# Top-32 attention followed by a mixture of experts on one core: VectorE's steps of a tile ordered by a list scheduler, and the mask added on GpSimd in every third tile

## The chip, the core and the metric

The kernel runs on one core of a Trainium2 chip. The metric is device microseconds (us) of one execution; the runs before the change lie between 1251.29 and 1252.31 us. The engines are called as in the profile: PE (TensorE matmul, with PEld for its weight loads), DVE (VectorE), ACT (ScalarE), POOL (GpSimd) and SP (the engine that issues most DMAs).

## What is computed

For 8 batches of 8 heads, 576 x 576 attention scores are formed; in each row only the 32 largest count, the rest are masked before the softmax. The result, 4608 rows of 512, goes through a mixture of 8 experts of which each row takes one.

```python
scores = scale * np.matmul(q, k.transpose(0, 1, 3, 2))      # per head, 576 x 576
kth = np.partition(scores, -top_k, axis=-1)[..., -top_k:-top_k + 1]
scores = np.where(scores >= kth, scores, -1000000000.0)
attn = np.exp(scores - np.max(scores, axis=-1, keepdims=True))
attn = attn / (np.sum(attn, axis=-1, keepdims=True) + 1e-09)
x = attn @ v                                                # 4608 rows of 512 in all
...
e_idx = np.argmax(x @ w_gate + modality_bias[modality_id], axis=1)
for e in range(E):
    h = np.maximum(x[mask] @ w1[e], 0.0)
    out[mask] = gate_w[mask, None] * (h @ w2[e])
```

## The kernel before

The scores are cut into 288 tiles of 128 rows by 576 columns, nine for each pair of heads, 36 for each batch. One pass of the main loop, an iteration `i`, works on several tiles at different stages, and the order in which the code emits instructions is the order in which each engine executes them. In iteration `i`:

- PE forms the scores of tile `i+2` in PSUM (`qk`, L368) and transposes the probabilities of tile `i-9` (`trans`, L476); between these it multiplies by `v` (L504) and takes matmuls of the expert layer (L775, L787) from a queue. How many it takes is set by a credit, `spare_pe`, that grows by `STEP` in every iteration.
- ACT copies the scores to SBUF as `Ssb` (`sevac`, L373; there are ten such buffers, so tile `i+2` needs the buffer of tile `i-8`), computes a sign map `K` (`sign`, L412), exponentials (L436) and the evacuation of the transposes (L484).
- POOL multiplies scores by the sign map, `y` (`pool_y`, L418, tile `i-4`), and prepares small values (`n` L405, `sm` L399).
- DVE finds the threshold. For tile `i`, six MAX8 over 96 columns each give 48 candidates (`subs`, L380). For tile `i-1` a chain of five dependent steps takes the 24 largest of the candidates: MAX, MATCH_REPLACE, MAX, MATCH_REPLACE, MAX (`chain`, L391 to L393). For tile `i-5` one MAX8 over `y` gives the next 8 (`find`, L422). In every third iteration three small dependent steps, `eq`, `jk` and `kth`, select the threshold of three tiles (`pick`, L429 to L431). Steps of routing and of the experts' schedule (`small_`) and multiplications that read PSUM (`lo`) come in between. Last in the iteration, the mask is applied to tile `i-7`.

The mask has two forms. In the usual one ACT computes `ex` = exp of all scores (`expo`) and DVE keeps those at or over the threshold in one instruction with two SBUF tensors as inputs, which also sums them (`keep`, L442). A one-element POOL instruction that reads its result (`gate`, L465) stands ahead of POOL's `y`, so that `y` starts when `keep` has ended. In the other form, chosen by `early`, DVE writes a large negative number where the score is under the threshold (`hide`, L449, one tensor input), POOL adds it to the scores (`hidden`, L455, at the top of the next iteration), and ACT takes the exponential of that and sums (`masked`, L461). That form has no gate. Before, `early` holds for two of three of the first 48 tiles, 32 tiles in all; the map lies in `hT`, a buffer that the experts need later.

DVE's order in an iteration is made by hand: `weave` spreads the steps of `b_` (candidates, `find`, `lo`) evenly behind those of the chain, up to four steps of `b_` are held back (`HOLD`) to stand between the small and pick steps of `c_`, and the mask comes last.

After tile 287 the experts' last seven slots run alone, in a split form with three matmuls for each product.

Of the kernel before, what the change touches and what calls it, by code (L numbers as in the profile page):

```python
# [11 lines left out]
BF = mybir.dt.bfloat16  # L12
# [11 lines left out]
NB = 4  # L24
LX = 13
SN = 4
KB = 2
LOP = (2, 5, 8, 10, 12)
NW = 3
STEP = 3.25  # L30
STEPS = {"small": 0.1, "late": 0.5, "more": 0.15}
LJ = (5, 6)
PJ = (0, 1, 3)
VJ = 7
QL = 2
HOLD = 4
KW = 8
FILL = 6
KL = 2
# [1 line left out]
LT = LY + 1  # L41
# [20 lines left out]
END = (-3, 1.0)  # L62
SP_ = (0, 0, 0, 0, 0)
HUGE = float(2.0 ** 100)
EARLY = 48
EPS = 1e-9
KTH_MIN, KTH_MAX = 1e-18, float(2.0 ** 26)
XW = 516
# [4 lines left out]
def kernel(  # L73
# [14 lines left out]
    B, H, S, D = q.shape  # L88
# [20 lines left out]
    wk = att.enter_context(tc.tile_pool(name="wk", bufs=3))  # L109
# [83 lines left out]
    hT = const.tile([128, FC, SLOT], FT, name="hT")  # L193
# [76 lines left out]
    late, late_pe = [], []  # L270
# [106 lines left out]
    def subs(i):  # L377
        c = wk.tile([128, NSUB * 8], FT, name="cand", bufs=2)
        T[i]["c"] = c
        return [lambda s=s: V.max(c[:, s * 8:s * 8 + 8], T[i]["S"][:, bnd[s]:bnd[s + 1]]) for s in range(NSUB)]  # L380

    def chain(i):
        if i % 3 == 0:
            T[i]["mg"] = wk.tile([128, 3, 32], FT, name="mg", bufs=5)
        else:
            T[i]["mg"] = T[i - 1]["mg"]
        m = T[i]["mg"][:, i % 3]
        c = T[i]["c"]
# [31 lines left out]
    def find(i):  # L420
        t = T[i]
        V.max(t["mg"][:, i % 3, 24:32], t["y"])  # L422

    def pick(i):

        t = T[i]
        eq, v = (wk.tile([128, 3, 9], FT, name=nm, bufs=1) for nm in ("eq", "jk"))
        n = t["n"][:, 0, :]
        return [lambda: V.tensor_tensor(eq, i9s, n[:, :, None].to_broadcast([128, 3, 9]), op=OP.is_equal),  # L429
                lambda: V.tensor_tensor(v, eq, t["mg"][:, :, 23:32], op=OP.mult),  # L430
                lambda: V.tensor_reduce(kth[:, i - 2:i + 1], v, axis=AX.X, op=OP.add)]  # L431
# [6 lines left out]
    def keep(i, dn):  # L438

        t = T[i]  # L440
        probs(i)
        V.scalar_tensor_tensor(t["P"], t["S"], kth[:, i:i + 1], t["ex"], op0=OP.is_ge, op1=OP.mult, accum_out=dn)  # L442

    def hide(i):

        t = T[i]
        x = 2 * (i % 2)
        t["hb"] = hT[:, x:x + 2, :].rearrange("p f t -> p (f t)").bitcast(BF)[:, :S]
        V.tensor_scalar(t["hb"], t["S"], kth[:, i:i + 1], -HUGE, op0=OP.is_lt, op1=OP.mult)  # L449

    def hidden(i):
# [15 lines left out]
    def probs(i):  # L467

        c, h = divmod(role(i), 2)
        T[i]["P"] = Pm[:, :S] if c == 4 else Pb[c % 2][:, h * S:h * S + S]  # L470
# [15 lines left out]
    def av(p, j, x):  # L486

        vm, vt = LD[p]["v"]
        w = 256 if j < 8 else 64
        st = {}  # L490

        def part(c0, c1):
            if c0 == 0:
                st["po"] = psX.tile([128, 256], FT, name="X")
            po = st["po"]
            for c in range(c0, c1):
                for h in range(2):
                    l = vm[:, h, c, :] if c < 4 else vt[:, h if j < 8 else 2 * h, :]
                    if j < 8:
                        r = PT[:, j // 2 - 1:j // 2 + 1, c + 5 * h if c < 4 else 4, :]  # L500
                    else:
                        r = PT[:, 1, 4 + c, h * 64:h * 64 + 64]
                    o = po[h * 64:h * 64 + 64, :w]
                    PE.matmul(o.rearrange("p (a b) -> p a b", a=2) if j < 8 else o, l, r, start=(c == 0), stop=(c == 4))  # L504
            if c1 == 5:
                o = (j // 4) * 256
                xev.append(lambda: A.activation(x[:, o:o + w], po[:, :w], AF.Copy))
        cut = {3: AV3, 7: AV7, 8: (0, 5)}[j]
        return [((b - a) * COST["av" if j < 8 else "av8"], lambda a=a, b=b: part(a, b)) for a, b in zip(cut, cut[1:])]
# [118 lines left out]
    after = deque()  # L628
# [265 lines left out]
                rush.extend(pick + [begin] + rows + l1[:1] + done + [PAUSE, l1[1], PAUSE, l1[2], l1[3], PAUSE] + tok + go)  # L894
            side.extend(l2)

    def weave(a, b):

        nb, na, kb = len(b), len(a), 0
        for x in range(na):  # L900
            a[x]()
            e = (x + 1) * nb // na
            while kb < e:
                b[kb]()
                kb += 1
        while kb < nb:
            b[kb]()
            kb += 1

    def keep_warm(n):  # L910

# [8 lines left out]
    def bounds():  # L920

        bt = wk.tile([128, S], BF, name="K", bufs=KB).bitcast(FT)[:, :NT]
        V.tensor_scalar(bt, kth, KTH_MIN, 0.0, op0=OP.is_le, op1=OP.add, accum_out=bd_[:, 0:1])
        V.tensor_scalar(bt, kth, KTH_MAX, 0.0, op0=OP.is_ge, op1=OP.add, accum_out=bd_[:, 1:2])

    def beyond():

        bb = bd_.bitcast(BF)[:, 4:6]
        V.tensor_scalar(bb, bd_[:, 0:2], 0.0, None, op0=OP.is_gt)
        pbad = psX.tile([128, 2], FT, name="X")  # L930
        PE.matmul(pbad, onesb, bb, start=True, stop=True)
        V.tensor_reduce(bd_[:, 3:4], pbad, axis=AX.X, op=OP.add)
        V.tensor_copy(badi, bd_[0:1, 3:4])
# [14 lines left out]
            qk(0, 0, qbd[0])  # L948
        sevac(x)
    ok = lambda x: 0 <= x < NT  # L950
    early = lambda u: u < EARLY and u % 3 != 2
    dn_of = lambda u: den[(u // 36) % 2][:, (u // 9) % HP, role(u):role(u) + 1]
    PREP, PREP0 = dict(zip(PJ, "tkq")), dict(zip(PJ0, "tkq"))
    two = lambda nm, shape: [wk.tile(shape, FR, name=nm + x) for x in "hl"]
# [105 lines left out]
    for i in range(LAST):  # L1060
# [8 lines left out]
        p, j = divmod(i, 9)  # L1069
        u = i - TL  # L1070
# [14 lines left out]
        u = i - (KL + 1)  # L1085
# [6 lines left out]
        u = i - LE  # L1092
# [6 lines left out]
        u = i - TL  # L1099
        if ok(u):  # L1100
            evac(u)
        u = i - LR - 1
        if ok(u) and early(u):
            masked(u, dn_of(u))
        lo, lp = list(late), list(late_pe)
# [7 lines left out]
        part = (PREP if p else PREP0).get(j)  # L1113
# [54 lines left out]
        if i == NT + LR + 4:  # L1168
            beyond()
        spare_pe = min(spare_pe + (STEP if i < NT + TL + END[0] else END[1]) - cost, CAP)  # L1170
        while seen[0] and spare_pe > 0:
# [4 lines left out]
            c, f, new = moe[0]  # L1176
# [10 lines left out]
                nxt.append(lambda u=i + QL: sevac(u))  # L1187


        a_, b_, c_ = [], [], []  # L1190
        if ok(i):
            b_ += subs(i)
        if ok(i - 1):
            a_ += chain(i - 1)
        if ok(i - LT):
            b_.insert(2, lambda: find(i - LT))
            if (i - LT) % 3 == 2:
                c_ += pick(i - LT)
        for x, f in enumerate(lo):
            b_.insert(LOP[x] if x < len(LOP) else len(b_), f)  # L1200
        small_ = []
        for x in range(RN if rush else 0):
            f = rush.popleft() if rush else PAUSE
# [3 lines left out]
        if not small_:  # L1207
            while chore:
                small_.append(chore.popleft())
        for x in range(SN - len(small_)):  # L1210
            f = side.popleft() if side and not rush else PAUSE
# [1 line left out]
                break  # L1213
            small_.append(f)
        spare_pe += STEPS["small"] * len(small_) + (STEPS["late"] + STEPS["more"] * (len(lo) - 1) if lo else 0.0)
        for x, f in enumerate(small_):
            c_.insert(2 * x, f)
        if ok(i - LR):
            u = i - LR
            c_.append(lambda u=u: hide(u) if early(u) else keep(u, dn_of(u)))  # L1220

        if ok(i) and len(c_) > 1:
            n = min(len(c_) - 1, HOLD)
            held, b_ = b_[len(b_) - n:], b_[:len(b_) - n]
            m = len(c_) - n
            c_ = c_[:m] + [f for pair in zip(held, c_[m:]) for f in pair]
        weave(a_, b_)
        for f in c_:
            f()

        for f in moves:
            f()
# [19 lines left out]
        if i == CLOSE:  # L1252
# [5 lines left out]
            wk = att.enter_context(tc.tile_pool(name="tl", bufs=1))  # L1258
# [53 lines left out]
    wk = att.enter_context(tc.tile_pool(name="wkb", bufs=3))  # L1312
# [101 lines left out]
```

## Time and profile before

| | |
|---|---|
| median of 3 runs | 1251.63 us (1251.29 to 1252.31) |
| profiled execution, its own time | 1250.95 us |
| its span, first to last instruction | 1249.3 us |
| busy share of the span | PE 93%, DVE 90%, ACT 80%, POOL 53% |

A row of the profile's groups gives line, engine, operation, output<-input, count, then busy microseconds and mean nanoseconds of one. A row of the timeline gives start and duration in microseconds. An instruction's duration there includes the end of its pipeline, so that the next one can start before the duration is over: what an instruction costs its engine is the distance from its start to the next start.

### The profile page before, as it was taken

The page shows a single profiled execution, that of the slowest core. Times are in us where ns is not written, and L with a number is a line of the kernel's source. Part 1 is how long each engine was busy: PE and PEld are TensorE (multiplying, and loading weights), DVE is VectorE, ACT ScalarE, POOL GpSimd, SP SyncE. Part 2 cuts the span into 40 slices and gives each one's busy share as a digit, 9 for nine tenths or more (in the row PEclk, how much of TensorE's full clock was granted, in tenths as well). Part 3 has the DMA queues.
Part 4 walks back from the last instruction along what each step waited for, and adds up shares of the span by engine and source line. Part 5 has one row for each costly group of instructions (what it writes and reads, how often), then busy time and mean ns, then how long its engine had stood idle before and what let it go on. Part 6 is the DMA issues. An engine that isn't in the chain of part 4 may idle for free.

```text
span 1249.3 us, 28363 instructions
## 1 busy us (share of the span) xinstructions
PE 1167.8 (93%) x7998; PEld 918.1 (73%) x7998; DVE 1129.0 (90%) x5596; ACT 995.1 (80%) x2026; POOL 661.0 (53%) x1256
## 2 busy tenths in 40 slices
PE   8888887999998998999999999999999999999995
PEld 6666666777866877677776868777786866799895
DVE  6999999999999999999999999999999993667761
ACT  4999987889898988988899889978998873545542
POOL 4888866455474557554755566546655561110110
PEclk6999999999999999999999999999999999999998
DMA  4664337655347655665656567556663543757650
GB/s 96 152 182 101 85 85 206 167 158 167 85 135 210 195 148 145 172 175 146 185 151 180 135 172 192 149 145 177 190 169 101 158 142 116 268 199 257 220 180 15
DMA packets 204325, 197.12 MB, mean 158 GB/s; under 512 B 104413, under 2 KB 151533, under 8 KB 204160
## 3 DMA queue, kind: packets, MB, share of 16 engines
q1 hardware_dynamic: 196880, 175.92, 51.3%
q0 software_dynamic: 6080, 19.00, 4.2%
q8 instruction: 67, 1.10, 0.4%
q14 instruction: 98, 0.80, 0.2%
q10 hardware_dynamic: 1200, 0.30, 0.1%
HBM read 118.63 MB, written 24.23 MB: 114 GB/s over the span
## 4 chain that ended last, share of the span: by engine, by line
DVE 47%; PE 39%; ACT 4%; issue 3%; DMA 3%; POOL 2%; SPq 0%; POOLq 0%; ACTq 0%
DVE cand L380 12%; DVE mg L422 9%; DVE P L442 8%; PE E L787 7%; PE X L1024 5%; PE E L775 5%; PE X L1008 4%; PE X L504 4%; PE S L368 4%; PE T L476 3%; DVE cand L391 3%; DVE cand L392 3%; DVE mg L393 2%; DVE mg L391 2%; DVE mg L392 1%
## 5 line engine op out<-in xcount | busy, mean ns | idle before, releaser
L380 DVE MAX8 cand<-Ssb 128x8 f32<-128x96 f32 x1728 | 402.0, 247 | 6.8 <-ACT Ssb L373 6.8
L418 POOL TENSOR_TENSOR y<-Ssb,K 128x576 f32<-128x576 f32 x288 | 367.5, 1276 | 6.2 <-ACT K L412 6.0
L412 ACT ACTIVATE K<-Ssb,n 128x576 bf16<-128x576 f32 x288 | 229.1, 796 | 18.9 <-POOL y L418 17.6
L373 ACT ACTIVATE Ssb<-S 128x576 f32<-128x576 f32 x284 | 187.1, 659 | 68.7 <-PE S L368 28.3
L368 PE MATMUL S<-ks,qs 128*128 128x288 f32 x992 | 219.4, 343 | 22.5 <-ACT Ssb L373 20.1
L422 DVE MAX8 mg<-y 128x8 f32<-128x576 f32 x288 | 214.3, 744 | 1.3 <-POOL y L418 1.2
L368 PEld LDWEIGHTS S<-ks,qs 128*128 128x128 f32 x992 | 151.0, 190 | 73.7 <-ACT Ssb L373 39.2
L436 ACT ACTIVATE ex<-Ssb,sm 128x576 f32<-128x576 f32 x256 | 201.6, 788 | 0.0
L484 ACT ACTIVATE PT<-T 128x640 f32<-128x640 f32 (+1 forms) x288 | 192.5, 668 | 6.4 <-PE T L476 6.4
L775 PE MATMUL E<-xgT,w1b 128*128 128x256 f32 x768 | 187.4, 386 | 6.4 <-ACT hT L779 5.0
L442 DVE SCALAR_TENSOR_TENSOR P<-Ssb,kth,ex 128x576 f32<-128x576 f32 x230 | 190.9, 830 | 1.0 <-ACT ex L436 0.8
L476 PE MATMUL T<-idf,P 128*128 128x128 f32 x1152 | 169.8, 274 | 7.4 <-ACT P L461 6.7
L787 PE MATMUL E<-w2b,hT 128*128 128x512 f32 x368 | 173.6, 601 | 1.8 <-ACT hT L779 1.6
L775 PEld LDWEIGHTS E<-xgT,w1b 128*128 128x128 f32 x768 | 140.4, 191 | 29.4 <-ACT hT L779 9.1
L465 POOL TENSOR_SCALAR spare<-P 1x1 f32<-1x1 f32 x230 | 42.0, 182 | 223.7 <-DVE mg L391 184.7
L504 PE MATMUL X<-PT,vm 128*64 128x256 f32 (+1 forms) x1536 | 145.3, 331 | 4.0 <-ACT st L282 2.8
L476 PEld LDWEIGHTS T<-idf,P 128*128 128x128 f32 x1152 | 137.0, 140 | 15.1 <-ACT P L461 11.0
L504 PEld LDWEIGHTS X<-PT,vm 128*64 128x64 f32 x1536 | 87.5, 137 | 49.1 <-issue 9.2
L405 POOL TENSOR_SCALAR n<-mg 128x1 f32<-128x1 f32 x288 | 71.1, 247 | 73.6 <-DVE mg L393 60.0
L787 PEld LDWEIGHTS E<-w2b,hT 128*128 128x128 f32 x368 | 65.8, 192 | 57.8 <-issue 52.4
L1030 POOL DMA_INDIRECT out_dram<-ot,tk x14 | 14.0, 998 | 116.2 <-ACT ot L1029 116.2
L412 ACT ACTIVATION_READ_ACCUMULATOR K<-Ssb,n 128x1 f32 x288 | 62.7, 218 | 0.0
(235 smaller groups left out, 2285.5 us busy)
## 6 DMA issues: line engine op xcount, KB each, us to landing
w1b<-in_moe_w_dram SPq DMA_DIRECT2D x76, 512.0 KB
w2b<-in_moe_w_dram SPq DMA_DIRECT2D x76, 512.0 KB
ks<-st SPq DMA_DIRECT2D x62, 288.0 KB
ks<-st SPq DMA_DIRECT2D x62, 256.0 KB
qs<-st SPq DMA_DIRECT2D x124, 128.0 KB
xg<-xs SPq DMA_DIRECT2D x19, 516.0 KB
km<-in_k_dram SPq DMA_DIRECT2D x64, 128.0 KB
vm<-in_v_dram SPq DMA_DIRECT2D x32, 256.0 KB
```

The costliest lines, as they stand in the source:

```text
L368: PE.matmul(ps[:, hf, :288], l, m, start=(n == 0), stop=(n == len(terms) - 1))
L380: return [lambda s=s: V.max(c[:, s * 8:s * 8 + 8], T[i]["S"][:, bnd[s]:bnd[s + 1]]) for s in range(NSUB)]
L412: A.activation(t["K"], t["S"], AF.Sign, scale=2.0 ** -24 - 1.0, bias=t["n"][:, 1, i % 3:i % 3 + 1], accum_out=t["n"][:, 0, i % 3:i % 3 + 1])
L418: G.tensor_tensor(t["y"], t["S"], t["K"], op=OP.mult)
L422: V.max(t["mg"][:, i % 3, 24:32], t["y"])
L436: A.activation(t["ex"], t["S"], AF.Exp, bias=t["s"][:, i % 3:i % 3 + 1])
L442: V.scalar_tensor_tensor(t["P"], t["S"], kth[:, i:i + 1], t["ex"], op0=OP.is_ge, op1=OP.mult, accum_out=dn)
L476: PE.transpose(T[i]["pt"][:, x, :], (Pm if c == 4 else Pb[c % 2])[:, h * 512 + x * 128:h * 512 + x * 128 + 128], idf)
L484: A.activation(o, T[i]["pt"][:, :n], AF.Copy)
L504: PE.matmul(o.rearrange("p (a b) -> p a b", a=2) if j < 8 else o, l, r, start=(c == 0), stop=(c == 4))
L775: PE.matmul(ps[:, f % 2], w1b[:, c, f * 128:(f + 1) * 128], xgT[:, c, :], start=(c == 0), stop=(c == KC - 1))
L787: PE.matmul(o["py"], hT[:, f, t * 128:(t + 1) * 128], w2b[:, f, :], start=(f == 0), stop=(f == FC - 1))
```

## The change

A table `USE` gives for each kind of DVE step two numbers, the time that it holds the engine and the time until its result may be used; `FROM` gives a kind the earliest place in the iteration. `arrange` then picks, step by step, among the steps whose inputs are ready the one with the longest path behind it. The mask (`end`) stays last, and behind the pick and the chain's last step. `early` now holds for every third tile of all 288, 96 in all; the map has a buffer of its own, `hb`. `STEP` goes from 3.25 to 3.2.

```diff
+USE = {"part": (0.165, 0.25), "max": (0.11, 0.235), "drop": (0.19, 0.3), "find": (0.667, 0.8), "pick": (0.086, 0.21), "late": (0.6, 0.75), "small": (0.09, 0.24), "keep": (0.726, 0.85)}
+FROM = {"late": 0.7, "pick": 1.5}
...
-STEP = 3.25
+STEP = 3.2
...
-        x = 2 * (i % 2)
-        t["hb"] = hT[:, x:x + 2, :].rearrange("p f t -> p (f t)").bitcast(BF)[:, :S]
+        t["hb"] = wk.tile([128, S], BF, name="hb", bufs=1)
         V.tensor_scalar(t["hb"], t["S"], kth[:, i:i + 1], -HUGE, op0=OP.is_lt, op1=OP.mult)
...
+    def arrange(ops, *last):
+
+        left, t, path = list(ops), 0.0, {}
+        ops = ops + list(last)
+        for o in reversed(ops):
+            path[o] = o.delay + max([path[x] for x in ops if o in x.after], default=0.0)
+        while left or last:
+            if not left:
+                left, last = list(last), ()
+            free = [o for o in left if not any(x in left for x in o.after)]
+            now = [o for o in free if o.start <= t + EPS]
+            o = max(now, key=lambda o: path[o]) if now else min(free, key=lambda o: o.start)
+            left.remove(o)
+            t = max(t, o.start)
+            for x in left:
+                if o in x.after:
+                    x.start = max(x.start, t + o.delay)
+            t += o.use
+            o.f()
...
-    early = lambda u: u < EARLY and u % 3 != 2
+    early = lambda u: u % 3 == 0
...
+            ops += run(("max", "drop", "max", "drop", "max"), chain(i - 1))
+        cut_ = ops[-1:]
...
+            ops += [Op("part", f) for f in subs(i)]
...
+            found = Op("find", lambda: find(i - LT))
...
-        weave(a_, b_)
-        for f in c_:
-            f()
+            end.append(Op("keep", lambda: hide(u) if early(u) else keep(u, dn_of(u)), got, *cut_))
+        arrange(ops, *end)
```

The first place is DVE in the iteration that masks tile 174, in the experts' part of the loop; `mg` holds the values found, `cand` with a number the candidates with the larger ones replaced. Before:

```order
L391 MAX mg<-cand 128x8
L391 MATCH_REPLACE cand_10999<-mg,cand 128x48
L380 MAX cand<-Ssb 128x8
L392 MAX mg<-cand_10999 128x8
L392 MATCH_REPLACE cand_11000<-mg,cand_10999 128x48
L380 MAX cand<-Ssb 128x8
L393 MAX mg<-cand_11000 128x8
L422 MAX mg<-y 128x8
L429 TENSOR_TENSOR eq<-i9s,n 128x27
```

The same start of that iteration after the change (line numbers are one lower there):

```order
L390 MAX mg<-cand 128x8
L421 MAX mg<-y 128x8
L390 MATCH_REPLACE cand_11036<-mg,cand 128x48
L379 MAX cand<-Ssb 128x8
L391 MAX mg<-cand_11036 128x8
L379 MAX cand<-Ssb 128x8
L391 MATCH_REPLACE cand_11037<-mg,cand_11036 128x48
L428 TENSOR_TENSOR eq<-i9s,n 128x27
L379 MAX cand<-Ssb 128x8
L429 TENSOR_TENSOR jk<-eq,mg 128x27
L392 MAX mg<-cand_11037 128x8
```

Between each MAX and the MATCH_REPLACE that needs its result now stands a step that needs neither; the MAX over `y` has moved up to second place. Counted over the main loop, the first MATCH_REPLACE stood right behind its MAX in 146 of 288 iterations and the second one in 73; now that is so in 0 and 1. Pairs of dependent small steps with nothing between them go from 57 to 9.

The second place is POOL, four iterations at the same part of the program. Before:

```order
L405 TENSOR_SCALAR n<-mg 128x1
L399 TENSOR_SCALAR sm<-mg 128x3
L465 TENSOR_SCALAR spare<-P_119 1x1
L418 TENSOR_TENSOR y<-Ssb,K 128x576
L405 TENSOR_SCALAR n<-mg 128x1
L465 TENSOR_SCALAR spare<-P_120 1x1
L418 TENSOR_TENSOR y<-Ssb,K 128x576
```

And after the change:

```order
L404 TENSOR_SCALAR n<-mg 128x1
L398 TENSOR_SCALAR sm<-mg 128x3
L453 TENSOR_TENSOR ex<-Ssb,hb 128x576
L417 TENSOR_TENSOR y<-Ssb,K 128x576
L404 TENSOR_SCALAR n<-mg 128x1
L463 TENSOR_SCALAR spare<-P_120 1x1
L417 TENSOR_TENSOR y<-Ssb,K 128x576
```

In one iteration of three the gate is replaced by a whole 128x576 addition, and `y` stands behind that. On PE, ACT and SP the kinds and counts stay, but for the exponentials that change form with the mask and six of PE's filler matmuls. The expert matmuls that PE has been given by tile 280 number 688 before and 684 after, counting a 512-wide one twice.

## Rows read from the trace of the kernel before

**Rows 1.** The page, parts 1 and 4: busy time, and the chain that ended last.

```profile
PE 1167.8 (93%) x7998; PEld 918.1 (73%) x7998; DVE 1129.0 (90%) x5596; ACT 995.1 (80%) x2026; POOL 661.0 (53%) x1256
...
DVE 47%; PE 39%; ACT 4%; issue 3%; DMA 3%; POOL 2%; SPq 0%; POOLq 0%; ACTq 0%
```

**Rows 2.** Busy time of each engine in stretches of the span, instructions in brackets.

```profile
39.00:151.00 112.00, 99.11 (x807) 77.70 (x805) 111.59 (x589) 105.58 (x239) 94.81 (x128) 0.99 0.51 133
...
221.00:1017.00 796.00, 764.12 (x5197) 587.63 (x5193) 783.09 (x4144) 699.73 (x1444) 463.34 (x918) 1.00 0.59 160
1017.00:1249.00 232.00, 216.88 (x1353) 183.30 (x1353) 138.46 (x357) 111.09 (x178) 35.88 (x80) 0.98 0.52 177
```

**Rows 3.** Waits of DVE: total us, times, longest us.

```profile
DVE cand L380 <- ACT Ssb L373: 6.8, 6, 2.2
...
DVE mg L422 <- POOL y L418: 1.2, 3, 0.6
```

**Rows 4.** Timeline of DVE, two iterations side by side, from 229 us.

```profile
229.41 0.19 DVE L391 MAX8 mg<-cand 128x8 f32<-128x48 f32 x1
229.54 0.23 DVE L380 MAX8 cand<-Ssb 128x8 f32<-128x96 f32 x1
...
230.03 0.18 DVE L392 MAX8 mg<-cand 128x8 f32<-128x48 f32 x1
230.14 0.73 DVE L422 MAX8 mg<-y 128x8 f32<-128x576 f32 x1
...
231.73 0.79 DVE L442 SCALAR_TENSOR_TENSOR P<-Ssb,kth,ex 128x576 f32<-128x576 f32 x1
...
232.45 0.20 DVE L391 MAX8 mg<-cand 128x8 f32<-128x48 f32 x1
232.68 0.09 DVE L391 MATCH_VALUE_LOAD cand<-mg,cand 128x8 f32 x1
```

**Rows 5.** Timeline of DVE, the experts' small steps, without and with a step between.

```profile
538.05 0.17 DVE L659 MAX8 s_m<-s_key 128x8 f32<-128x8 f32 x1
538.25 0.23 DVE L670 TENSOR_SCALAR s_oh<-s_key,s_m 128x8 f32<-128x8 f32 x1
...
495.85 0.17 DVE L659 MAX8 s_m<-s_key 128x8 f32<-128x8 f32 x1
495.93 0.24 DVE L380 MAX8 cand<-Ssb 128x8 f32<-128x96 f32 x1
```

**Rows 6.** Timeline of all engines from 100 us: both forms of the mask, and POOL.

```profile
100.94 0.70 DVE L449 TENSOR_SCALAR hT<-Ssb,kth 128x576 bf16<-128x576 f32 x1
...
103.03 1.29 POOL L418 TENSOR_TENSOR y<-Ssb,K 128x576 f32<-128x576 f32 x1
...
103.87 1.06 DVE L442 SCALAR_TENSOR_TENSOR P<-Ssb,kth,ex 128x576 f32<-128x576 f32 x1
...
107.59 0.50 DVE L449 TENSOR_SCALAR hT<-Ssb,kth 128x576 bf16<-128x576 f32 x1
...
108.01 0.20 DVE L391 MAX8 mg<-cand 128x8 f32<-128x48 f32 x1
...
108.18 1.29 POOL L455 TENSOR_TENSOR ex<-Ssb,hT 128x576 f32<-128x576 f32 x1 [0.47 <-DVE hT L449]
...
109.43 1.29 POOL L418 TENSOR_TENSOR y<-Ssb,K 128x576 f32<-128x576 f32 x1
```

**Rows 7.** Timeline of POOL and of DVE at 878 us.

```profile
878.63 1.27 POOL L418 TENSOR_TENSOR y<-Ssb,K 128x576 f32<-128x576 f32 x1
...
878.77 1.74 DVE L442 SCALAR_TENSOR_TENSOR P<-Ssb,kth,ex 128x576 f32<-128x576 f32 x1
```

**Rows 8.** Groups by line on ACT: the sum that the other mask form reads out.

```profile
L461 ACT ACTIVATION_READ_ACCUMULATOR P<-ex,sm 128x1 f32 x26 | 5.9, 226 | 0.0
```

**Rows 9.** Timeline of PE: transposes, and the group that starts behind them.

```profile
617.19 0.71 PE L476 MATMUL T<-idf,P 128*128 128x128 f32 x5
617.65 0.48 PE L281 MATMUL X<-st,nid 128*128 128x512 f32 x1
```

More of the change, by code (lines that the diff above doesn't have):

```diff
@@ L26 @@
 SN = 4
+USE = {"part": (0.165, 0.25), "max": (0.11, 0.235), "drop": (0.19, 0.3), "find": (0.667, 0.8), "pick": (0.086, 0.21), "late": (0.6, 0.75), "small": (0.09, 0.24), "keep": (0.726, 0.85)}
+FROM = {"late": 0.7, "pick": 1.5}
 KB = 2
-LOP = (2, 5, 8, 10, 12)
 NW = 3
-STEP = 3.25
+STEP = 3.2
 STEPS = {"small": 0.1, "late": 0.5, "more": 0.15}
@@ L35 @@
 QL = 2
-HOLD = 4
 KW = 8
@@ L64 @@
 HUGE = float(2.0 ** 100)
-EARLY = 48
 EPS = 1e-9
@@ L895, in more_moe, with __init__, run @@
             side.extend(l2)
[L897 to L908, printed above, removed]
+    class Op:
+        def __init__(self, kind, f, *after):
+            self.f, self.after = f, [o for o in after if o is not None]
+            self.use, self.delay = USE[kind]
+            self.start = FROM.get(kind, 0.0)
+    def run(kind, fs, *after):
+        ops = []
+        for f in fs:
+            ops.append(Op(kind if isinstance(kind, str) else kind[len(ops)], f, *(ops[-1:] or after)))
+        return ops
+    def arrange(ops, *last):
[16 more added lines that the diff above has]
+            o.f()
     def keep_warm(n):
@@ L1187 @@
                 nxt.append(lambda u=i + QL: sevac(u))
-        a_, b_, c_ = [], [], []
+        ops, found, got = [], None, None
+        if ok(i - 1):
+            ops += run(("max", "drop", "max", "drop", "max"), chain(i - 1))
+        cut_ = ops[-1:]
         if ok(i):
-            b_ += subs(i)
-        if ok(i - 1):
-            a_ += chain(i - 1)
+            ops += [Op("part", f) for f in subs(i)]
         if ok(i - LT):
-            b_.insert(2, lambda: find(i - LT))
+            found = Op("find", lambda: find(i - LT))
+            ops.append(found)
             if (i - LT) % 3 == 2:
-                c_ += pick(i - LT)
-        for x, f in enumerate(lo):
-            b_.insert(LOP[x] if x < len(LOP) else len(b_), f)
+                e_, v_, s_ = pick(i - LT)
+                e_ = Op("pick", e_)
+                v_ = Op("pick", v_, e_, found)
+                got = Op("pick", s_, v_)
+                ops += [e_, v_, got]
+        ops += run("late", lo)
         small_ = []
@@ L1215 @@
         spare_pe += STEPS["small"] * len(small_) + (STEPS["late"] + STEPS["more"] * (len(lo) - 1) if lo else 0.0)
-        for x, f in enumerate(small_):
-            c_.insert(2 * x, f)
+        ops += run("small", small_)
+        end = []
         if ok(i - LR):
             u = i - LR
[L1220 to L1226, printed above, removed]
-        weave(a_, b_)
-        for f in c_:
-            f()
+            end.append(Op("keep", lambda: hide(u) if early(u) else keep(u, dn_of(u)), got, *cut_))
+        arrange(ops, *end)
         for f in moves:
```

## The prediction, made before the changed kernel ran

> **What bounds the kernel now.** I read the busy shares and the chain that ended last, then the busy time by stretches, then DVE's waits, then the distances between starts on DVE. Over the whole span PE is the busiest engine with 93%, but the chain runs through DVE for 47% and PE for 39% [rows 1]. The stretches part these. From 39 to 151 us, where most of the first 48 tiles run, DVE is busy 111.59 of 112 us; from 221 to 1017 us, where 224 tiles and most of the expert matmuls run, it is busy 783.09 of 796 us; from 1017 us on the last expert slots run, DVE is busy only 138.46 of 232 us and PE 216.88 [rows 2]. So DVE sets the pace of the loop up to 1017 us and PE sets that of the tail. DVE hardly waits for others in the loop: 6.8 us for scores in all, 1.2 us for `y` [rows 3].
>
> A busy DVE is not yet a DVE at its peak, and that is the heart of this change. A MAX of the chain that is followed by work that doesn't need it gives way after 0.13 us (229.41 to 229.54) or 0.11 us (230.03 to 230.14); one followed by the MATCH_REPLACE that needs it (its first part is the MATCH_VALUE_LOAD) holds the engine 0.23 us (232.45 to 232.68) [rows 4]. This waiting is counted as busy.
>
> **The change, part by part.** All prices are distances between starts on DVE.
>
> *Order of the chain.* 146 + 73 direct pairs of MAX and MATCH_REPLACE become 1. The distance falls from 0.23 us to 0.13 or 0.11 us, so each saves 0.10 to 0.12 us, 22 to 26 us in all; I take the middle, 218 x 0.11 = 24 us.
>
> *Order of the small steps.* 57 pairs become 9. A dependent one follows 0.20 us behind (538.05 to 538.25), an independent one 0.08 us behind (495.85 to 495.93) [rows 5]: 48 x 0.12 = 5.8 us. Some of it may only move to another wait, so its lower end is 0.
>
> A rule of the Trainium skill speaks against both of these terms. The page "VectorE: DVE Perf Modes", in the section "The DRAIN you can't avoid", says that after every VectorE instruction the next one doesn't start until the pipeline is empty, and that chaining without waits in between gains nothing. By that rule the two terms would be 0. The trace doesn't agree for these instructions: the MAX at 229.41 lasts 0.19 us and the next one starts 0.06 us before its end [rows 4]. So I keep the 24 and 5.8 us, and the rule becomes a rival below.
>
> *Mask on POOL in 96 tiles instead of 32.* For 64 more tiles DVE does `hide` instead of `keep`. `keep` holds DVE 0.72 us (231.73 to 232.45) [rows 4], `hide` 0.42 us (107.59 to 108.01) [rows 6]: 64 x 0.30 = 19.2 us.
>
> *What POOL's addition costs DVE.* While POOL runs one of its 128x576 instructions, DVE's mask is slow. `keep` takes 1.06 us at 103.87, with `y` on POOL until 104.32, against 0.79 us alone [rows 4, 6]; with `y` beside its first 1.13 us it takes 1.74 us [rows 7]. `hide` takes 0.70 us at 100.94, beside the end of a `y`, against 0.50 us at 107.59 [rows 6]. Before, in two of three of the first 48 tiles, this hits 14 `keep` at 0.27 us and 13 `hide` at 0.20 us, counted as the masks that stand one iteration behind a `hide`: 3.8 + 2.6 = 6.4 us, which goes away, since no `hide` follows a `hide` any more and the `keep` behind one is counted now. After the change one `keep` in three iterations stands behind a `hide`. POOL's addition starts 0.17 us after `hide` ends (108.01 to 108.18), `y` follows 1.25 us later (109.43) and ends 1.29 us after that [rows 6], 2.71 us into the iteration. An iteration without small steps lasts 3.04 us (229.41 to 232.45) and its `keep` starts 0.72 us before its end [rows 4], at 2.32 us: 0.39 us of overlap, about as at 103.87 (0.45 us). So I take the same 0.27 us for those iterations behind a `hide` that have few or no steps besides; by the program's order these are 62. Price: 62 x 0.27 = 16.7 us. From below it is 0, if everything is a little later on DVE than I count; from above all 96 pay, 26 us.
>
> *`find` in second place.* It now needs `y` at 0.13 us into the iteration, instead of after one or two further steps. In a usual iteration `y` has ended long before. Behind a POOL addition it ends at 2.71 us, and the iteration lasts 3.04 us or, with the slow `keep`, 3.3 us. So 0.45 us are left, and I put it at 0. If that cover is gone, every 0.1 us in each of 96 iterations costs 9.6 us.
>
> *ACT and PE.* The other exponential adds a read of the sum, 226 ns [rows 8]: at most 64 x 0.23 = 14.5 us of ACT time, over a loop in which ACT is busy 699.73 of 796 us [rows 2]. It lies beside DVE's work as long as ACT stays under DVE: 714 us against DVE's 796 less the gains. PE's filler is unchanged in amount. PE is shown busy for 764.12 of the 796 us, but its shown times overlap: five transposes at 617.19 are shown for 0.71 us, and the next group starts after 0.46 us [rows 9]. So PE has more room than the 32 us that the row leaves, and how much more the rows don't say. With POOL's addition the tile's `Ssb` buffer comes free 1.4 us later than with `keep`, which delays ACT's copy, and with it PE's next scores; the scores are two iterations ahead, so I take this as hidden. For all such coupling I take 4 us, between 0 and 28 us; the upper end is my choice of how much of the sum could go: all but some 10 us of it.
>
> *The sum.* 24 + 5.8 + 19.2 + 6.4 - 16.7 - 4 = 34.7 us, nearly all of it between 221 and 1017 us; in the first 48 tiles `hide` gets rarer, and the terms cancel. The tail after 1017 us only moves forward. The profiled execution took 1250.95 us in all, 1.65 us more than its span, and 0.7 us less than the median of the runs. So 1250.95 - 34.7 + 0.7 = 1217 us.
>
> **The rivals.**
> *POOL's second instruction disturbs less or not at all:* small steps, late multiplications and waits make the iterations longer than 3.04 us (the mean over 221 to 1017 us is 796 / 224 = 3.55 us [rows 2]), and then `keep` starts after `y` has ended. For: only a part of the iterations is bare. Against: those I counted are bare ones. Then 16.7 and 4 us stay: 1217 - 20.7 = 1196 us, or a little more where some is left.
> *PE takes over as the bound:* it is shown busy 764.12 of 796 us [rows 2], and a PE that is full can't follow. For: the row. Against: the overlap in [rows 9]. If the loop is held up so that a third to two thirds of the sum are lost, 12 to 23 us, the time is 1229 to 1240 us, 1235 us in the middle.
> *The order gives nothing:* what is left is 19.2 + 6.4 - 16.7 = 8.9 us, 1243 us. This is what the page's rule on the drain would give. Against it stand the distances in [rows 4].
> *Slower:* `y` slides under the whole `keep` in the iterations behind POOL's addition. A full overlap costs 1.74 - 0.79 = 0.95 us [rows 4, 7], and with 96 of them 91 us, 74 us more than I count: 1217 + 74 = 1291 us. The point from which the change loses is an average of 0.36 us more than I count in each of the 96 (34.7 / 96), that is, `y` about 0.45 us later than 2.71 us on average. For: POOL's indirect DMAs and other small work stand on its queue behind `y`, and one late one put `y` under `keep` at 878.63 [rows 7]. Against: a slow `keep` lengthens its own iteration, and POOL then has 3.3 us for 2.71 us of work, so that delays don't add up. The Trainium skill names the cause: "GPSIMD Engine Reference", section "Specifications", says that GpSimd shares its SBUF interfaces with VectorE instructions that have two SBUF inputs or run in a two-port mode. By that page alone any mask of DVE pays whenever POOL runs, which is what [rows 6] show for both forms.
> *No change:* the gains vanish in waits of equal size.
>
> **How the numbers follow.** The forecast, 1203 to 1229 us, has 0.55; less disturbance, 1190 to 1203 us, 0.10; PE as the bound, 1229 to 1241 us, 0.18; order without effect, around 1243 us, 0.05; no change 0.04; slower 0.08. The range is to leave out about 2 in 10: 1202 us leaves out most of the second case, 1242 us the last three and a part of the fourth. A measurement of this kernel tells about 0.2%, 2.5 us, from no change. Faster by more: 0.55 + 0.10 + 0.18 + 0.05 = 0.88; within: 0.04; slower: 0.08.
>
> **What would show it.** Right: bare iterations of DVE stay near 3.04 us, those with a pick and `hide` last about 3.0 us, and no MATCH_REPLACE follows its MAX by 0.23 us. `keep` behind a `hide` lasts about 1.06 us in some 62 iterations and 0.8 us elsewhere. The last tile's merge comes about 35 us earlier than 1017 us, and the tail behind it keeps its 232 us. Wrong: DVE waits for `Ssb` or `y` by tens of us, where it waited 6.8 and 1.2 us [rows 3]; `keep` at 1.3 us and more in many iterations; or a tail that grows as the loop shrinks.

## The result, and the profile of the changed kernel

The changed kernel takes 1263.08 us (median of 4 runs, 1262.24 to 1263.73), the kernel before 1251.61 us (4 runs). The ratio is 1.0098, with a 95% interval of 1.0081 to 1.0116: it is 1.0% slower. The forecast was 1217 us, with a range of 1202 to 1242 us; the sign was wrong and the time lies outside the range. The profiled execution has a span of 1260.3 us, where before it was 1249.3 us.

The page of the changed kernel, parts 1 and 4 (they answer to [rows 1]):

```profile
PE 1176.0 (93%) x7992; PEld 923.7 (73%) x7992; DVE 1128.5 (90%) x5532; ACT 998.2 (79%) x2090; POOL 753.1 (60%) x1256
...
DVE 58%; PE 27%; POOL 5%; issue 4%; DMA 3%; ACT 3%; SPq 0%; POOLq 0%; ACTq 0%
```

DVE has 64 instructions fewer and is just as busy as before: 1128.5 against 1129.0 us. Its share of the chain that ended last has grown from 47% to 58%. So what was saved on DVE came back on DVE, in instructions that last longer.

Busy time by stretches (for [rows 2]):

```profile
39.00:151.00 112.00, 97.64 (x803) 78.54 (x802) 112.00 (x603) 104.98 (x228) 81.97 (x128) 0.97 0.51 133
221.00:1017.00 796.00, 762.70 (x5164) 585.91 (x5161) 776.09 (x4028) 698.53 (x1508) 561.53 (x909) 0.99 0.59 159
1017.00:1260.00 243.00, 227.12 (x1391) 188.76 (x1389) 145.33 (x397) 118.07 (x194) 43.64 (x89) 0.98 0.51 173
```

The waits of DVE (for [rows 3]):

```profile
DVE mg L421 <- POOL y L417: 21.7, 9, 4.4
DVE cand L379 <- ACT Ssb L372: 4.6, 3, 2.2
```

PE and ACT are no busier between 221 and 1017 us than they were. DVE waits 21.7 us for `y` instead of 1.2, and for scores less than before.

The timeline of the changed kernel, DVE with POOL, at four places. It holds the main finding:

```profile
232.34 0.18 DVE L392 MAX8 mg<-cand 128x8 f32<-128x48 f32 x1
232.44 0.55 DVE L379 MAX8 cand<-Ssb 128x8 f32<-128x96 f32 x3
...
238.06 1.29 POOL L417 TENSOR_TENSOR y<-Ssb,K 128x576 f32<-128x576 f32 x1
...
238.98 0.98 DVE L441 SCALAR_TENSOR_TENSOR P<-Ssb,kth,ex 128x576 f32<-128x576 f32 x1
...
356.20 1.33 DVE L428 TENSOR_TENSOR eq<-i9s,n 128x27 f32<-128x27 f32 x1
356.21 1.28 POOL L417 TENSOR_TENSOR y<-Ssb,K 128x576 f32<-128x576 f32 x1
357.46 0.25 DVE L379 MAX8 cand<-Ssb 128x8 f32<-128x96 f32 x1
...
360.84 0.30 POOL L329 TENSOR_SCALAR qbd<-st 64x128 fp32r<-64x128 f32 x1 [3.08 <-DMA xs<-x,dest]
...
363.49 1.27 POOL L453 TENSOR_TENSOR ex<-Ssb,hb 128x576 f32<-128x576 f32 x1
364.72 1.28 POOL L417 TENSOR_TENSOR y<-Ssb,K 128x576 f32<-128x576 f32 x1
...
366.03 0.76 DVE L421 MAX8 mg<-y 128x8 f32<-128x576 f32 x1 [3.82 <-POOL y L417]
...
367.79 1.26 POOL L417 TENSOR_TENSOR y<-Ssb,K 128x576 f32<-128x576 f32 x1
367.93 0.18 DVE L392 MAX8 mg<-cand 128x8 f32<-128x48 f32 x1
368.04 1.04 DVE L653 SCALAR_TENSOR_TENSOR s_jk<-s_oh,s_av 128x8 f32<-128x8 f32 x1
369.02 0.57 DVE L379 MAX8 cand<-Ssb 128x8 f32<-128x96 f32 x3
```

At 232.34 the chain behaves as forecast: the next MAX starts 0.10 us behind. At 238.98 `keep` does too: it begins before `y` has ended (239.35) and lasts 0.98 us. At 356.20 stands what the forecast didn't have. `eq`, a step on 27 columns, starts as `y` does on POOL and lasts 1.33 us; `y` ends at 357.49, `eq` at 357.53. At 368.04 `s_jk`, on 8 columns, lasts 1.04 us: `y` ends at 369.05, it at 369.08. The MAX at 367.93 stands under the same `y` and lasts its usual 0.18 us. At 360.84 a filling of `qbd` on POOL waits 3.08 us for a transfer; the mask's addition and `y` stand behind it on POOL's queue, and `find` waits 3.82 us for `y`.

How such steps fare in all is read from the views by tile (duration ns as minimum/median/maximum). Of the changed kernel:

```profile
L656 DVE SCALAR_TENSOR_TENSOR s_key<-s_av,rev x19: 143/168/1159, 189.6 to 1197.8; 128x8 f32<-128x8 f32 x19
L657 DVE MAX8 s_m<-s_key x19: 145/156/171, 190.2 to 1198.0; 128x8 f32<-128x8 f32 x19
...
L653 DVE SCALAR_TENSOR_TENSOR s_jk<-s_oh,er x12: 142/166/1023, 194.7 to 1199.2; 128x8 f32<-128x8 f32 x12
...
L428 DVE TENSOR_TENSOR eq<-i9s,n x96: 156/172/1333, 30.9 to 1037.0; 128x27 f32<-128x27 f32 x96
```

Of the kernel before, by tile, and below it a row of POOL's timeline:

```profile
L658 DVE SCALAR_TENSOR_TENSOR s_key<-s_av,rev x19: 166/168/236, 192.2 to 1186.8; 128x8 f32<-128x8 f32 x19
...
L430 DVE TENSOR_TENSOR jk<-eq,mg x96: 157/170/1300, 32.1 to 1028.4; 128x27 f32<-128x27 f32 x96
```

```profile
749.04 0.30 POOL L330 TENSOR_SCALAR qbd<-st 64x128 fp32r<-64x128 f32 x1 [2.92 <-DMA xs<-x,dest]
```

The medians are equal; the maxima aren't. I call a step held where it lasts over 0.3 us and ends within 0.1 us of the end of a 128x576 instruction of POOL that it began under. Between 150 and 1060 us the small steps, with `jk` counted among them, show 8 held ones before, 6.9 us above 0.16 us each in all, and 68 after, 36.1 us. One `jk` of 1300 ns stood in the trace of before already: a row that the prediction didn't look for. The filling of `qbd` waited for its transfer before too (2.92 us at 749.04), while `find` waited 1.2 us in all [rows 3].

### The profile page after: what moved, and what is told of

Its sections match the earlier page's. It is cut to its first block, busy times and chain, and to the rows that moved or that the text cites. A ratio compares the mean times of both kernels' runs of the same rounds, so it can differ in the third digit from the quotient of the medians.

```text
span 1260.3 us, 28213 instructions
## 1 busy us (share of the span) xinstructions
PE 1176.0 (93%) x7992; PEld 923.7 (73%) x7992; DVE 1128.5 (90%) x5532; ACT 998.2 (79%) x2090; POOL 753.1 (60%) x1256
## 4 chain that ended last, share of the span: by engine, by line
DVE 58%; PE 27%; POOL 5%; issue 4%; DMA 3%; ACT 3%; SPq 0%; POOLq 0%; ACTq 0%
DVE cand L379 16%; DVE mg L421 10%; DVE P L441 9%; PE X L1043 5%; PE X L1027 4%; PE E L773 4%; DVE cand L390 3%; DVE cand L391 3%; PE E L785 3%; DVE hb L447 2%; DVE mg L392 2%; DMA xs<-x,dest 2%; PE X L502 2%; DVE mg L390 2%; DVE mg L391 2%
## 5 line engine op out<-in xcount | busy, mean ns | idle before, releaser
L379 DVE MAX8 cand<-Ssb 128x8 f32<-128x96 f32 x1728 | 371.9, 241 | 4.6 <-ACT Ssb L372 4.6
L417 POOL TENSOR_TENSOR y<-Ssb,K 128x576 f32<-128x576 f32 x288 | 368.1, 1278 | 9.5 <-ACT K L411 9.3
L367 PE MATMUL S<-ks,qs 128*128 128x288 f32 x992 | 218.5, 342 | 36.1 <-ACT Ssb L372 35.0
L421 DVE MAX8 mg<-y 128x8 f32<-128x576 f32 x288 | 212.6, 738 | 21.7 <-POOL y L417 21.7
L773 PE MATMUL E<-xgT,w1b 128*128 128x256 f32 x768 | 190.1, 390 | 6.7 <-ACT hT L777 5.3
L441 DVE SCALAR_TENSOR_TENSOR P<-Ssb,kth,ex 128x576 f32<-128x576 f32 x192 | 172.4, 898 | 1.0 <-ACT ex L435 1.0
L773 PEld LDWEIGHTS E<-xgT,w1b 128*128 128x128 f32 x768 | 142.1, 194 | 31.4 <-ACT hT L777 10.2
L435 ACT ACTIVATE ex<-Ssb,sm 128x576 f32<-128x576 f32 x192 | 151.8, 790 | 0.0
L453 POOL TENSOR_TENSOR ex<-Ssb,hb 128x576 f32<-128x576 f32 x96 | 123.7, 1289 | 44.3 <-DVE hb L447 41.1
L404 POOL TENSOR_SCALAR n<-mg 128x1 f32<-128x1 f32 x288 | 81.8, 284 | 106.8 <-DVE mg L392 68.1
L463 POOL TENSOR_SCALAR spare<-P 1x1 f32<-1x1 f32 x192 | 35.0, 182 | 115.2 <-DVE mg L390 99.4
```

What stands on the lines that cost most here:

```text
L367: PE.matmul(ps[:, hf, :288], l, m, start=(n == 0), stop=(n == len(terms) - 1))
L417: G.tensor_tensor(t["y"], t["S"], t["K"], op=OP.mult)
L773: PE.matmul(ps[:, f % 2], w1b[:, c, f * 128:(f + 1) * 128], xgT[:, c, :], start=(c == 0), stop=(c == KC - 1))
```

## The experiments

Two explanations are told apart below. *Contention*: a DVE step with two SBUF inputs that starts while POOL runs a 128x576 instruction does not end before that instruction does. *Coupling*: PE or ACT hold the loop, and DVE's long steps only show where the time is spent.

This table splits, for five of the kernels, the time from the first MAX of the chain of the 61st tile (its first merge) to that of the last tile. Each group has the distances from its instructions' starts to the next start on DVE, without the waits that the trace shows; those stand apart. All are worked out from the timeline of DVE, in us.

| | before | mask rule alone | order alone | changed kernel | order behind y |
|---|---|---|---|---|---|
| chain of MAX and MATCH_REPLACE | 181.0 | 180.8 | 156.2 | 156.2 | 156.2 |
| masks (`keep`, `hide`) | 168.1 | 157.4 | 166.0 | 157.4 | 166.9 |
| small steps | 35.0 | 51.2 | 54.5 | 57.8 | 37.3 |
| pick (`eq`, `jk`, `kth`) | 20.4 | 26.1 | 23.2 | 29.1 | 30.3 |
| candidates, `find`, late | 398.1 | 396.3 | 393.8 | 393.8 | 394.2 |
| waits for `y` | 1.2 | 7.2 | 11.4 | 15.8 | 3.0 |
| other waits | 3.5 | 4.5 | 1.3 | 5.0 | 1.2 |
| sum | 807.3 | 823.5 | 806.4 | 815.1 | 789.1 |

**The two halves of the change.** The order alone, with the old rule and the old place of the hidden mask:

```diff
-    early = lambda u: u % 3 == 0
+    early = lambda u: u < 48 and u % 3 != 2
```

> The list scheduler with the mask's old rule (two thirds of the first 48 tiles). Contention theory: the order alone saves some 24 us on the chain and loses some 25 to 30 us on small steps under y: 1248 to 1260 us. If the mask rule is what costs the time, the order alone gives 1220 to 1235 us.

Measured: 1252.52 us, ratio to before 1.0018 (1.0003 to 1.0034), within the band of contention. The mask rule alone, on the kernel before:

```diff
-    early = lambda u: u < EARLY and u % 3 != 2
+    early = lambda u: u % 3 == 0
```

with a buffer of its own for the hidden mask, as in the change.

> The hand-made order with GpSimd adding the mask in every third tile. Contention theory: 20 us saved by hide, 6 us of old conflicts gone, 10 to 17 us of new ones on keep: 1238 to 1248 us. If the mask rule is what costs the time: over 1256 us.

Measured: 1269.83 us, 1.0160 (1.0136 to 1.0183). This is not the band that contention on `keep` alone gave; it is the other one. So neither half makes the kernel faster by itself. The order gains its 24.8 us in the chain and gives 19.5 back in small steps and 10.2 in waits for `y`. The mask rule gains 10.7 us in the masks and gives 16.2 back in small steps, 5.7 in the pick and 6.0 in waits for `y`: in its iterations `y` runs 1.25 us later, behind the addition, and so over the end of the iteration, where the old order has the small steps (35 held ones, 21.7 us).

**Only the small steps later, only `find` later.** In the changed kernel, one number each in the planner's earliest times:

```diff
-FROM = {"late": 0.7, "pick": 1.5}
+FROM = {"late": 0.7, "pick": 1.5, "small": 1.5}
```

> The change, but small steps may not be placed before 1.5 us of an iteration. Contention theory (VectorE's small steps with two SBUF inputs, moved ahead, are held until GpSimd's y ends at about 1.45 us): of some 39 us that small and pick steps hold VectorE longer than before, 25 or more go, and the time is 1230 to 1242 us. Coupling theory (PE or ACT hold the loop, and the long small steps only show where the time is spent): 1257 to 1264 us.

Measured: 1259.77 us, 1.0076 (1.0052 to 1.0099).

```diff
-FROM = {"late": 0.7, "pick": 1.5}
+FROM = {"late": 0.7, "pick": 1.5, "find": 1.2}
```

> The change, but the MAX over y may not be placed before 1.2 us of an iteration. If its early place costs what its waits show (about 16 us against 1.5 us before): 1246 to 1254 us. If those waits only move elsewhere: 1258 to 1264 us.

Measured: 1279.98 us, 1.0245 (1.0219 to 1.0271). By their numbers both speak against contention: the first falls where the rival put it, the second lies above both of its bands. The traces tell why neither edit is the test I took it for. With the small steps from 1.5 us on, those of an iteration behind a POOL addition still start under `y`, which there runs until 2.7 us: 37 held steps instead of 68, but longer ones, 27.9 us. With `find` moved away, the steps that stood behind it move up under `y`: 60 held ones, 50.7 us. The waits of DVE for scores, which the rival needs, don't grow in the first: waits other than for `y` are 6.2 us there, 5.0 in the changed kernel.

**Both behind `y`, with the old mask rule.** Order alone, with:

```diff
-FROM = {"late": 0.7, "pick": 1.5}
+FROM = {"late": 0.7, "pick": 1.5, "find": 1.2, "small": 1.5}
```

> The new order with the old mask rule (as in the run with the order alone, 1252.5 us), and in it the small steps from 1.5 us into the iteration on and find from 1.2 us on, so that both stand behind the usual end of y. Contention theory: in the 224 - 32 iterations without a mask on GpSimd nothing with two SBUF inputs starts under y any more; small steps fall from 58 to some 34 us and find's waits from 13 to 2 us, 1220 to 1236 us. Rival (coupling: TensorE and ScalarE can't follow a faster VectorE): VectorE's steps get cheaper but its waits for scores grow, not under 1245 us.

Measured: 1231.28 us (4 runs), 0.9842 (0.9817 to 0.9866). This beats both kernels: 20 us less than before, 32 us less than the changed kernel. Its page, part 4, its waits of DVE for `y`, its stretch from 221 us on and its `s_key`:

```profile
PE 47%; DVE 38%; ACT 5%; DMA 3%; issue 3%; POOL 2%; SPq 1%; POOLq 0%; DVEq 0%; ACTq 0%
```

```profile
DVE mg L421 <- POOL y L417: 4.6, 7, 1.3
```

```profile
221.00:980.00 759.00, 740.40 (x5080) 576.81 (x5077) 749.28 (x4046) 683.01 (x1416) 450.19 (x898) 1.00 0.62 165
```

```profile
L657 DVE SCALAR_TENSOR_TENSOR s_key<-s_av,rev x19: 142/154/170, 187.8 to 1166.1; 128x8 f32<-128x8 f32 x19
```

No `s_key` is held any more; 9 small steps are left that are (6.3 us). The chain keeps its 156.2 us. The pick is at 30.3 us for another reason than holding (in the stretch of the table two `eq` last over 0.3 us): in 41 of its 76 turns `kth` now has the mask that needs it right behind, and `kth` takes 14.4 us instead of 6.1. PE followed a loop that is 18 us shorter (789.1 against 807.3 us), and DVE's waits for others shrank: the rival of coupling is refuted down to this length. PE is shown busy for 740.40 of 759 us, so it may be near.

**The mask rule in that order.** The changed kernel with the same two numbers, and with small steps from 2.75 us on where a mask is added on POOL:

```diff
+        FROM["small"] = 2.75 if ok(i - 1 - LR) and early(i - 1 - LR) else 1.5
```

> The changed kernel (mask on GpSimd in every third tile) with find from 1.2 us on and the small steps from 1.5 us on, or from 2.75 us on in the iterations in which a mask addition and y run on GpSimd one after the other. Contention theory: small steps fall from 65 to some 40 us, but eq and the mask keep are still held in a third of the iterations (some 14 + 7 us) and find waits for y there; 1238 to 1252 us, so the mask rule loses against the old one in the same order. Rival (the loss is not from where the small steps stand, but from waits for scores on ScalarE and TensorE): 1258 us or more.

Measured: 1252.99 us, 1.0009 (0.9993 to 1.0024): just above the band that contention allowed, and 22 us more than with the old mask rule. From the 61st tile on small steps take 50.8 us (31 held ones, 14.4 us), waits 15.0 us, and the masks 161.0 us: of 192 `keep`, 65 last over 0.95 us. So the mask rule costs more than it saves in the better order too. No mask on POOL at all, in the order behind `y`:

```diff
-    early = lambda u: u < 48 and u % 3 != 2
+    early = lambda u: False
```

> The kernel with small steps and find behind y, with no mask on GpSimd at all: VectorE does keep in all 288 tiles. By the prices at 1 of 3 in every theory, 32 more keep cost 32 x 0.3 = 9.6 us and the conflicts of the first 48 tiles (some 6 us) go away: 1231 to 1238 us. If instead a mask on GpSimd costs more than it saves even in the first 48 tiles (y late behind it, find and eq under y): below 1229 us.

Measured: 1239.08 us, 0.9902 (0.9881 to 0.9923), just above the band of the first case; the second is refuted. The first 48 tiles, with hardly a small step beside them (0.9 us), take 152.2 us instead of 146.2. There a mask on POOL pays; later, beside small steps, it doesn't.

**The length of the hold.** The changed kernel with `y` in two halves:

```diff
-        G.tensor_tensor(t["y"], t["S"], t["K"], op=OP.mult)
+        for h in (0, S // 2):
+            G.tensor_tensor(t["y"][:, h:h + S // 2], t["S"][:, h:h + S // 2], t["K"][:, h:h + S // 2], op=OP.mult)
```

> The changed kernel with GpSimd's product y written as two instructions over 288 columns each instead of one over 576. Contention theory (a VectorE step with two SBUF inputs that starts while a GpSimd 128x576 instruction runs does not end before that instruction does): the steps are now held to the end of a half, so eq, whose longest are 1.33 us, and the small steps should last at most some 0.7 us when they start under y, and the time that small steps and eq take of VectorE between 221 and 1025 us (65 and 15 us in the changed kernel) falls by 10 to 25 us; GpSimd pays up to 0.2 us more for each y. Kernel 1240 to 1262 us. Rival (the small steps run slowly all along beside any GpSimd work, and it is the amount of GpSimd work that counts): their time stays, no step is shorter than before, 1263 us or more since GpSimd has more to do.

Measured: 1271.21 us, 1.0151 (1.0121 to 1.0181). The time lies where the rival put it. POOL is busy with `y` for 417.9 us, where 288 whole ones took 368.1: 0.17 us more for each, within the 0.2 us expected. But the waits for `y` grow from 15.8 to 27.0 us, and in the stretch of the table small steps and pick together take only some 3 us less, not 10 to 25: small steps gain 7 us, and the pick, of which 27 steps are held between 150 and 1060 us instead of 12, loses 4. The durations speak against the rival, which had no step shorter, and are as contention has them; the view by tile of this kernel:

```profile
L654 DVE SCALAR_TENSOR_TENSOR s_jk<-s_oh,s_av x12: 142/166/500, 193.6 to 1207.6; 128x8 f32<-128x8 f32 x12
...
L654 DVE SCALAR_TENSOR_TENSOR s_jk<-s_oh,er x12: 153/168/473, 196.4 to 1208.3; 128x8 f32<-128x8 f32 x12
```

The maxima are 500 and 473 ns instead of 1043 and 1023, the longest `eq` lasts 641 ns instead of 1333, and 62 held small steps cost 23.7 us instead of 36.1. So such a step is held to the end of the one instruction of POOL, not as long as POOL has work.

**The price of a held step by itself.** The kernel in the order behind `y`, with a step more in every third iteration that nobody needs, early (below) or late (1.7 instead of 0.6):

```diff
+FROM = {"probe": 0.6, "late": 0.7, "pick": 1.5, "find": 1.2, "small": 1.5}
+    probe = const.tile([128, E], FT, name="probe", bufs=1)
+        if ok(i) and ok(i - LT) and (i - LT) % 3 == 0:
+            ops.append(Op("probe", lambda: V.tensor_tensor(probe, ie, ie, op=OP.add)))
```

> The kernel with the old mask rule and small steps and find behind y (1231.3 us), and in every third iteration one more VectorE step that nothing waits for and that waits for nothing: an addition of a constant 128x8 tile to itself, placed 0.6 us into the iteration, under y. Contention theory: each of some 95 such steps is held until y ends, 0.6 to 0.9 us instead of 0.15 us, and the iteration gets that much longer: 60 to 85 us more, 1290 to 1316 us. Rival (a step costs its own start to start distance wherever it stands, and the loss of the changed kernel lies in waits for other engines): 95 x 0.09 = 9 us more, 1238 to 1242 us.

Measured: 1308.48 us, 1.0450 (1.0428 to 1.0472): 77.2 us more than without it.

> The same additional step, but 1.7 us into the iteration, behind y. Both theories: about 9 us more than without it, 1236 to 1246 us, with steps of 0.15 us. It is there to part the place from the step: if it also costs 60 us, the addition itself is dear and not its place.

Measured: 1246.45 us, 0.9953 (0.9935 to 0.9971): 15.2 us more. The early step, by tile and on the timeline:

```profile
L1227 DVE TENSOR_TENSOR probe<-ie x95: 146/1059/1187, 23.1 to 1069.4; 128x8 f32<-128x8 f32 x95
```

```profile
676.24 1.27 POOL L417 TENSOR_TENSOR y<-Ssb,K 128x576 f32<-128x576 f32 x1
...
676.47 1.07 DVE L1227 TENSOR_TENSOR probe<-ie 128x8 f32<-128x8 f32 x1
677.47 0.20 DVE L391 MAX8 mg<-cand 128x8 f32<-128x48 f32 x1
```

The late one:

```profile
L1227 DVE TENSOR_TENSOR probe<-ie x95: 136/148/797, 24.4 to 1008.3; 128x8 f32<-128x8 f32 x95
```

```profile
151.36 1.28 POOL L417 TENSOR_TENSOR y<-Ssb,K 128x576 f32<-128x576 f32 x1
...
151.95 0.71 DVE L1227 TENSOR_TENSOR probe<-ie 128x8 f32<-128x8 f32 x1
...
640.23 1.28 POOL L417 TENSOR_TENSOR y<-Ssb,K 128x576 f32<-128x576 f32 x1
...
641.83 0.15 DVE L1227 TENSOR_TENSOR probe<-ie 128x8 f32<-128x8 f32 x1
```

The same instruction costs 0.15 us behind `y` and 1.07 us under it. Of the 95 early ones 87 are held, 76.2 us above 0.15 us in all, and the kernel is 77.2 us longer: what is held comes out in the time in full. The late ones cost more than the 9 us of either theory, and the trace shows why: 16 of the 95, all before 185 us, where masks are still added on POOL, stand, as at 151.95, under a `y` that runs late behind a mask's addition (9.0 us). With 95 x 0.09 = 8.6 us that makes 17.6 us, for 15.2 measured.

**The waits at the fillings of `qbd`.** The changed kernel, with the mask on DVE in 8 of the 96 tiles, those whose addition stands behind a filling as at 360.84:

```diff
-    early = lambda u: u % 3 == 0
+    early = lambda u: u % 3 == 0 and u % 36 != 24
```

> The changed kernel, with the mask on VectorE in 8 of the 96 tiles: those whose addition stands on GpSimd's queue behind the filling of qbd, which waits for a transfer of xs there. Contention theory: in the changed kernel find waits some 16 us for y at five such places; without the addition y is 1.3 us earlier at each, find waits 5 to 9 us less in all, and 8 keep cost 2.4 us: 1255 to 1261 us, and the other 40 us of held steps stay. Rival (the waits at the fills are the main loss): 1250 us or less.

Measured: 1259.10 us, 1.0057 (1.0038 to 1.0076), 4 us less than the changed kernel. The waits for `y` fall from 15.8 to 10.1 us in the stretch of the table, the masks rise by 1.9 us, small steps stay (58.8 us). The addition lengthens these waits, but more than half of them stay without it, and they are not the main loss.

**STEP.** The order behind `y` with the planner's iteration at 3.25 us, as before:

```diff
-STEP = 3.2
+STEP = 3.25
```

> As the run with small steps and find behind y, with the planner's length of an iteration back at 3.25 from 3.2 (before has 3.25). If the new STEP costs (too few or too many small steps per iteration, a longer tail), this is 3 to 10 us faster than that run; if STEP plays no part, within 3 us of it.

Measured: 1230.91 us, 0.9840 (0.9815 to 0.9866), 0.4 us from that with 3.2. From the last tile's first merge to the end it takes 233.3 us instead of 235.9, and that merge comes 3.3 us later: STEP moves work between loop and tail and plays no part in the sum.

## Why the prediction was wrong

*Order of the chain: right.* Forecast -24 us; the chain falls from 181.0 to 156.2 us, -24.8. The rival that the order gives nothing is refuted. The prediction took it from a section of the Trainium skill, "The DRAIN you can't avoid" of "VectorE: DVE Perf Modes", and passed over a sentence of it: "A next op that is not held starts earlier" (held there means by VectorE's own earlier instructions, not by POOL). So that section did not speak against this term. The trace agrees with that sentence: at 232.34 a MAX lasts 0.18 us, and the next one starts 0.10 us behind its start.

*Masks: right.* `hide` and `keep` together were to bring -19.2 - 6.4 + 16.7 = -8.9 us over all tiles; by the way of the table they bring -9.0 over all tiles and -10.7 from the 61st on. `keep` was to be slowed in some 62 iterations by 0.27 us each; 62 of the 192 last over 0.95 us, by 19.3 us more than 0.8 us each. So the slower rival (all of `keep` under `y`) did not happen; it was the right mechanism on the wrong instructions.

*Small steps: the step that failed.* Forecast -5.8 us, with "its lower end is 0". Measured +22.8 us, and +8.7 us in the pick, which had no term (ten held `eq` and one `jk`). The prediction counted how many dependent pairs the new order parts, and gave the steps the price of a step where it stood before. But the order also moved them from the end of an iteration to its beginning, under `y`, and there a step doesn't cost 0.08 or 0.20 us but the rest of `y`. The mask rule does the same from the other side: behind the addition `y` runs later, over the old place of the small steps (16.2 us with that rule alone). [rows 6, 7] show just this for the masks, and I took it for a matter of wide tiles. The experiments with the added step show it by itself, and with the steps behind `y` 17.2 of the 19.5 us come back.

*`find` in second place: the second step that failed.* Forecast 0, with 0.45 us of cover behind a POOL addition. Waits for `y` rose by 14.6 us, all of it in five places 36 tiles apart (3.82 us at 366.03, the others 2.63, 2.62, 2.29 and 4.45 us). In four of them POOL's queue stands behind a filling that waits for a transfer, as it did before; what is new is that `find` comes earlier (order alone: 11.4 us) and that an addition stands ahead of `y` (mask rule alone: 7.2 us). The sensitivity was named (9.6 us for each 0.1 us in 96 iterations), but not POOL's queue at these places as what takes the cover away.

*Coupling to PE and ACT: right in size.* Forecast +4 us; other waits rose by 1.5. PE as the bound did not come: the order behind `y` runs the loop 26 us faster than the changed kernel, with the same work on PE.

*The tail* was to stay at 232 us; it takes 235.5 us (1260.3 - 1024.8). STEP moves some of this (235.9 to 233.3 us in the order behind `y`), and in that pair it came back in the loop.

From the 61st tile on this adds up to -24.8 - 10.7 + 22.8 + 8.7 + 14.6 + 1.5, and -4.3 in candidates, `find` and late multiplications: +7.8 us. With the tail's 3.3 us that is the 11 us by which the span grew. The Trainium skill has the rule that was missing, on another page than the one that the prediction cited: "SBUF — State Buffer", section "Who interferes with whom", says that VectorE's instructions with two SBUF inputs contend with GpSimd's that read SBUF, that those in a 2-port mode contend with GpSimd too, and that whoever issues first blocks the other fully for its whole instruction. The traces agree on VectorE's side: an 8-column step ends with the 1.28 us of `y`, and with its half where `y` is halved. They agree on GpSimd's side in the rows at 757.07 (last section). By that rule the width of the step plays no part, and I had priced it by width.

Open: with the mask rule in the order behind `y` small steps take 50.8 us, of which holding explains 14.4. The steps' own price is most of the rest (35.0 - 6.9 = 28.1 us before); some 8 us more are not explained in full. There 67 of the 296 small steps take 0.18 to 0.30 us until the next start, as one with a dependent step right behind does, against 53 before and 20 in the changed kernel.

## What to carry to other kernels

Before steps are moved on VectorE, look at what GpSimd runs at the new place: a tiny step with two SBUF inputs under a long GpSimd instruction costs the rest of that instruction, is shown as busy time and not as a wait, and, where VectorE sets the pace as here, comes out in the kernel's time in full. Read maxima of durations, not means; one 8-column step that lasts a microsecond tells the mechanism. A scheduler that knows only engine times and dependencies needs a window in which such steps may not start, and moving one kind of step out of it without the others pulls the others in.

## What the runs showed of the hardware that I had not expected

The hold doesn't depend on the size of VectorE's step: 128x8 (0.15 us alone) and 128x27 (0.17 us) last to 0.02 to 0.06 us behind the end of POOL's 128x576 instruction, up to 1.33 us. All 61 `keep` of the changed kernel that began at least 0.25 us ahead of the end of a 128x576 instruction of POOL ended 0.61 to 0.62 us behind that end, whether they had begun 0.36 or 1.18 us ahead of it; so did all 17 of the kernel before. Most of the 0.79 us of a `keep` is done only afterwards. One that began only 0.05 us ahead of an addition's end, with `y` right behind on POOL, was held to the end of `y` as well and lasted 1.9 us (at 204.46).

POOL waits likewise where DVE's step comes first. In the changed kernel an addition that started 0.11 us into a `keep` lasted 1.83 us, against 1.29 us on the mean:

```profile
757.07 0.80 DVE L441 SCALAR_TENSOR_TENSOR P<-Ssb,kth,ex 128x576 f32<-128x576 f32 x1
757.18 1.83 POOL L453 TENSOR_TENSOR ex<-Ssb,hb 128x576 f32<-128x576 f32 x1
```

The run with the mask off the places behind a filling has such a `y` at 658.33, 0.04 us into a `keep`: it lasts 1.91 us. No run was made for this alone.

Not held under POOL's instruction were MAX8 (0.18 us at 367.93, and 0.73 to 0.76 us for all 288 `find`), MATCH_REPLACE (0.19 us), TENSOR_REDUCE (0.16 us for `kth`, in and out of it), RECIPROCAL (0.17 us) and the late multiplications over 512 columns, of whose two inputs one lies in PSUM (0.68 us for 28 under it, 0.67 us for 4 that no such instruction touched). Some steps with a single SBUF tensor were held: `rd<-den` takes 0.63 instead of 0.16 us (means of 5 and 3), the copy `sgt<-xg` 0.75 instead of 0.15 (4 and 2). The traces don't show why these were and the others weren't.

POOL's `y` takes 1278 ns as a whole (mean) and, in two halves, 1418 ns from the start of the first to the end of the second (median): cutting it costs some 140 ns.
